# An early check set at a later place, four placing products for eight, and two subtractions on GpSimd

## The chip, the cores and the metric

The kernel runs on one core of a Trainium2 chip. TensorE (PE) multiplies matrices, VectorE (DVE), ScalarE (ACT) and GpSimd (POOL) do the elementwise work, SyncE (SP) and POOL issue transfers. The engines run on their own and meet at semaphores. The metric is the time of the whole program on the device in microseconds; the kernel before takes 439.84 us as the median of three runs (439.14 to 439.93).

## The reference

```python
x = A_x                                   # (1, 2048, 640)
xn = (x - mean(x)) / sqrt(var(x) + 1e-5)   # over the 640 channels
a = einsum("bsd,ed->bse", xn, dft_hid_re);  b = einsum("bsd,ed->bse", xn, dft_hid_im)
A = einsum("ts,bse->bte", dft_seq_re, a) - einsum("ts,bse->bte", dft_seq_im, b)
h = (xn - mean(xn)) / sqrt(var(xn) + 1e-5)
u = gelu(einsum("bsd,sf->bdf", h, w1) + b1)          # F = 1728
B = (einsum("bdf,fs->bds", u, w2) + b2).transpose(0, 2, 1)
out = x + A + B
```

The two DFT matrices along the sequence are 2048 x 2048, the two along the channels 640 x 640; all are inputs. Everything is float32.

## The kernel before

A float32 product is made of three passes in a faster format: each operand is cut into a high half (ACT copies it to the rounded type, `high`, L130) and a low half (DVE subtracts the high half from the source, `low`, L133), and PE multiplies high by high, high by low and low by high (`three`, L138 to L140).

The program is one list of steps. The first 16, called blocks here, take one row tile of x each (128 tokens by 640 channels) in the order of `k_order`, and multiply it with the weight pieces of the first four column groups of w1 into all eight PSUM banks: 24 products a block (`up_pass`, L301). A block needs its row normalized and cut (`row_high`, L245 and L130; `row_low`, L133), and before that the row's moments on DVE (L200, L203), a reciprocal root on ACT (`rooted`, L225) and four tiny instructions that refine it (`factors`, L229 to L232; on DVE for the first five rows, on POOL for the rest). There are 16 early weight pieces of 128 x 512, four for each group of four blocks, in eight buffers (tags h0 to h6 and cut0). The first four are loaded and cut in halves of 256 columns, since they are needed first. After block 15 come the gelus (`gelu`, L325), which read the eight banks on ACT, and step 16, whose products (L138) begin to write the first two of these banks again. Steps 16 and 17 use two further weight pieces ("piece"), cut during blocks 14 and 15.

Since the kernel uses symmetries of the DFT matrices, it checks that they hold: sixteen sets of columns are loaded and compared on DVE with their mirror images (L999, L1003, L1005, L1012), ACT squares what is left and adds it up (L1022), and at the end a verdict decides whether a general version has to run as well. The first seven sets are early ones. Set 0 loads a base and three further tiles of 0.5 MB each through SP; L999 compares the second tile, L1003 the third, L1005 the fourth, and L1012 the base with itself. In the kernel before it is loaded in blocks 4, 4, 5 and 6 and compared three blocks later, with buffers n6 and n7 and the base ck[0].

For the DFT part the row factors of the normalization have to lie in another order of rows: `all_factors` (L398 to L402) computes them for all rows, `norm_parts` cuts them, `norm_products` (L429) multiplies them with four 0/1 matrices on PE, and `norm_places` (L436 and POOL copies) puts them at their places in norm_pairs, which L470 reads later.

The order on each engine is the order in which the program emits its instructions: for every step it runs in turn the loads, the reads of PSUM, the high halves of a piece two steps ahead, the middle, the low half of that piece, the measures and what is to come behind them, and then the step's products. `set_at` puts a set's loads at the steps of a list and its comparisons `by` steps later. Every engine works its list in order, so an instruction that waits holds all behind it.

Of the kernel before, what the change touches and what calls it, by code (L numbers as in the profile page):

```python
# [8 lines left out]
F32 = mybir.dt.float32  # L9
# [3 lines left out]
AF = mybir.ActivationFunctionType  # L13
# [3 lines left out]
P = 128  # L17
S = 2048
D = 640
F = 1728  # L20
NS = S // P
# [18 lines left out]
FIRST = 4  # L40
# [9 lines left out]
def fnet_plus_mixer(  # L50
# [22 lines left out]
    nc = tc.nc  # L73
# [58 lines left out]
    def low(lo, src, hi):  # L132
        nc.vector.tensor_sub(lo, src, hi.bitcast(F32))  # L133
# [63 lines left out]
    def half_moments(k, i):  # L197
        if i == 0:
            stats[k] = small.tile([P, 2, 6], F32, name="st")
        nc.vector.bn_stats(stats[k][:, i, :], rows[k][:, i * H2 : (i + 1) * H2])  # L200
# [222 lines left out]
        low(norm_cut[:, 1], norm, norm_cut[:, 0])  # L423

    def norm_products():
        n = 2 * NS
        for c in range(4):
            for part in range(2):
                nc.tensor.matmul(  # L429
                    psum[6][:, c * n : (c + 1) * n], places[0][:, c // 2, c % 2], norm_cut[:, part].rearrange("p k c -> p (k c)"),  # L430
                    start=c == 0 and part == 0, stop=c == 3 and part == 1, skip_group_check=True,
                )

    def norm_places():
        of = ck[1][:, : 8 * NS]
        nc.scalar.activation(of, psum[6][:, : 8 * NS], AF.Copy)  # L436
        of = of.rearrange("p (s v h k c) -> p s v h k c", s=2, v=2, h=2, k=HS)
        to = norm_pairs.rearrange("p (h b j v) c -> p b v h j c", h=2, b=2, v=2)
        half = P // 2
        for v in range(2):  # L440
            for i in range(2):
                p = slice(half * i, half * (i + 1))
                nc.gpsimd.tensor_copy(to[p, 0, v], of[p, 0, v, :, i : i + 2 * NJ - 1 : 2])

            nc.gpsimd.tensor_copy(to[:, 1, v], of[:, 1, v, :, HS - 2 : HS - 1 - 2 * NJ : -2])
            p = slice(0, half + 1 - v)
            nc.gpsimd.tensor_copy(to[p, 1, v], of[p, 1, v, :, HS - 1 : HS - 2 * NJ : -2])
        nc.gpsimd.tensor_copy(to[0:1, 1, 0], of[0:1, 1, 0, :, NK : NK + 2 * NJ - 1 : 2])
# [582 lines left out]
    def set_at(u, when, by, base, places, late):  # L1031
        load, compare, compare_mirror = seq_set(u, base, places, late)
        for i in range(len(when)):
            at(when[i], load, i, when=loads)
            if i:
                at(when[i] + by, compare, i, when[i] + by, when=behind)
        at(when[-1] + by, compare_mirror, when[-1] + by, when=behind)
# [143 lines left out]
    def early_base(n):  # L1181
        return lambda: ck[(n + 1) % 2][:, : S // 2]
# [4 lines left out]
        return keep.tile([P, S // 2], F32, name=f"check{n}", tag=f"h{4 + i}")  # L1187


    first_ends = []  # L1190

    def first_place(i):
        if i != 1:
            first_ends.append(keep.tile([P, 2, S // 2], F32, name=f"check_first{i}", tag=f"n{6 + i // 2}"))
        return first_ends[-1][:, i % 2]

    set_at(sets[0], [4, 4, 5, 6], 3, early_base(1), first_place, 0)
    for n in range(1, n_early):
        i = n_first + 4 * (n - 1)
        when = [i, i, i + 1, i + 2] if n < n_early - 1 else [i, i, i + 1, i + 4]  # L1200
# [46 lines left out]
    with tc.manual_schedule():  # L1247
        for i in range(2):
            cols = slice(i * H2, (i + 1) * H2)
            nc.sync.dma_start(rows[k_order[0]][:, cols], x_rows[k_order[0]][:, cols])  # L1250
        for n in range(FIRST):
            w1_place(*first_pieces[n])


        def half_pieces(pair, part):
            cols = slice(part * 2 * P, (part + 1) * 2 * P)
            two = w1[2 * pair : 2 * pair + 2, groups[0], :, cols].rearrange("f p c -> p f c")
            nc.sync.dma_start(w_raw[:, pair, :, cols], two)  # L1258

        x_load(k_order[1])  # L1260
        half_pieces(0, 0)
        half_pieces(1, 0)
        for pair in range(2):
            half_pieces(pair, 1)
        for j in range(2, 6):
            x_load(k_order[j])
        for n in range(FIRST, 8):
            w1_load(*first_pieces[n])
        nc.gpsimd.iota(lanes, pattern=[[0, 2]], base=0, channel_multiplier=1)
        constants()  # L1270
        nc.gpsimd.dma_start(b1_sb, b1)
        nc.gpsimd.dma_start(b2_sb, b2)
        iotas()
        nc.scalar.activation(one, eps, AF.Abs_reciprocal_sqrt)

        def first_high(n, part):
            c = slice(part * 2 * P, (part + 1) * 2 * P)
            if part == 0:
                t = early_tile(n)
                w_cut[first_pieces[n]] = t[:, 0], t[:, 1]  # L1280
            high(w_cut[first_pieces[n]][0][:, c], w_at[first_pieces[n]][:, c])

        def first_low(n, part):
            c = slice(part * 2 * P, (part + 1) * 2 * P)
            hi, lo = (a[:, c] for a in w_cut[first_pieces[n]])
            low(lo, w_at[first_pieces[n]][:, c], hi)

        row = k_order[:5]
        moments(row[0])
        rooted(row[0])  # L1290
        factors(row[0])
        row_high(row[0], True)
        for n in range(2):
            first_high(n, 0)
        moments(row[1])
        rooted(row[1])
        for n in range(2, FIRST):
            first_high(n, 0)
        half_low(row[0], 0)
        factors(row[1])  # L1300
        half_low(row[0], 1)
        row_high(row[1], True)
        first_low(0, 0)
        row_low(row[1])
        for n in range(1, FIRST):
            first_low(n, 0)
        mean_by_scalar(row[2])
        variance_by_scalar(row[2])
        rooted(row[2])
        for n in range(FIRST):  # L1310
            first_high(n, 1)
        half_moments(row[3], 0)
        factors(row[2])
        row_high(row[2], True)
        half_moments(row[3], 1)
        joined(row[3])
        row_low(row[2])
        mean_by_scalar(row[4])
        rooted(row[3])
        variance_by_scalar(row[4])  # L1320
        factors(row[3])
        row_high(row[3])
        rooted(row[4])
        for n in range(FIRST):
            first_low(n, 1)
        row_low(row[3])
        factors(row[4])

        for i in range(n_steps + 1):
            j = i + AHEAD  # L1330
            all_of(loads, i)
            if not s_seq <= i < s_hid:
                all_of(reads, i)
            if j < n_steps and steps[j][0]:
                steps[j][0]()
            all_of(reads, i)
            all_of(middle, i)
            if j < n_steps and steps[j][1]:
                ready[j] = steps[j][1]()
            all_of(measures, i)  # L1340
            all_of(behind, i)
            if i < n_steps:
                steps[i][2](ready.pop(i, None))
# [136 lines left out]
```

## Time and profile before

| | |
|---|---|
| median of 3 runs | 439.84 us (439.14 to 439.93) |
| profiled execution, its own time | 439.92 us |
| span from the first to the last instruction | 438.1 us |
| mean granted PE clock | 0.997 |
| PE busy | 430.7 us, 98% |
| DVE busy | 326.1 us, 74% |
| ACT busy | 247.1 us, 56% |
| POOL busy | 108.6 us, 25% |
| blocks 0 to 15 on PE | 7.45 to 66.65 us |

A row of the timeline gives the start, the time taken, the engine, the line, the operation, what is written and read, and in brackets how long the engine stood idle before it and what ended that. A row of the list of waits gives the total in us, the number and the longest. A row of a table of stretches gives the stretch, its length, the busy time of PE with the number of instructions that touch it, the granted clock, the DMA share and GB/s. Matmuls are pipelined: their durations overlap, and the distance between their starts is what a stretch of them costs.

### The profile page before, as it was taken

What the parts mean: (1) busy time and instruction counts of PE and PEld (TensorE: products, weight loads), DVE (VectorE), ACT (ScalarE), POOL (GpSimd) and SP (SyncE); (2) the same over time, 40 slices, a digit from 0 to 9 for tenths busy, and PEclk for the clock granted to TensorE, in tenths of its full rate; (3) what the DMA queues carried; (4) which work ended last, traced back from release to release, by engine and by line L of the source; (5) the groups of instructions that cost most, each with busy time, mean ns of one, the idle gap of its engine ahead of it and who ended that gap; (6) DMA issues with size and microseconds to landing.
All of it is one profiled execution on the core that took longest, in us unless ns stands there. A gap on an engine that the chain in (4) does not pass through costs nothing.

```text
span 438.1 us, 8076 instructions
## 1 busy us (share of the span) xinstructions
PE 430.7 (98%) x2963; PEld 424.4 (97%) x2963; DVE 326.1 (74%) x665; ACT 247.1 (56%) x476; POOL 108.6 (25%) x164
## 2 busy tenths in 40 slices
PE   9999999999999999999999999999999999999994
PEld 5999999999999999999999999999999999999994
DVE  7887861578777777795888759989778677869671
ACT  5967955566556646475946424556645555545540
POOL 2056511032220001100002425546434516312000
PEclk9999999999999999999999999999999999999998
DMA  8992347597886561233203799999999988996301
GB/s 271 339 373 101 104 180 272 178 322 269 279 287 226 194 222 57 72 99 95 101 23 122 212 339 397 389 396 364 404 402 399 399 315 287 407 328 240 113 31 38
DMA packets 43839, 105.68 MB, mean 241 GB/s; under 512 B 5748, under 2 KB 7940, under 8 KB 43792
## 3 DMA queue, kind: packets, MB, share of 16 engines
q1 hardware_dynamic: 34816, 72.66, 46.5%
q0 software_dynamic: 8832, 32.27, 20.2%
q8 instruction: 25, 0.41, 0.4%
q14 instruction: 22, 0.18, 0.1%
q10 hardware_dynamic: 144, 0.16, 0.1%
HBM read 94.58 MB, written 10.49 MB: 240 GB/s over the span
## 4 chain that ended last, share of the span: by engine, by line
PE 87%; DMA 3%; DVE 3%; ACT 2%; POOL 2%; issue 1%; SPq 1%; POOLq 0%; ACTq 0%
PE psum L138 26%; PE psum L140 26%; PE psum L139 26%; PE psum L301 4%; PE psum L897 2%; PE psum L290 2%; DMA xp<-in_x 1%; ACT zt L245 1%; DMA xm<-in_x 1%; POOL r L230 1%; DVE st L200 1%; DVE x L133 1%; DVE early L133 0%; SPq L1258 0%; ACT x L130 0%
## 5 line engine op out<-in xcount | busy, mean ns | idle before, releaser
L133 DVE TENSOR_TENSOR piece<-w_raw,piece 128x512 fp32r<-128x512 f32 (+2 forms) x128 | 76.5, 598 | 80.3 <-ACT piece L130 75.6
L130 ACT ACTIVATE piece<-w_raw 128x512 fp32r<-128x512 f32 (+2 forms) x112 | 67.0, 600 | 110.1 <-PE psum L140 73.4
L138 PE MATMUL psum<-x,piece 128*128 128x320 f32 x288 | 89.1, 309 | 0.0
L140 PE MATMUL psum<-x,piece 128*128 128x320 f32 x288 | 89.1, 309 | 0.0
L139 PE MATMUL psum<-x,piece 128*128 128x320 f32 x288 | 88.8, 308 | 0.0
L1022 ACT ACTIVATE check<-check 128x1024 f32<-128x1024 f32 (+2 forms) x62 | 61.4, 991 | 32.5 <-DVE check L1005 14.2
L140 PE MATMUL psum<-h_cut,piece 128*128 128x320 f32 x256 | 79.2, 310 | 0.0
L138 PE MATMUL psum<-h_cut,piece 128*128 128x320 f32 x256 | 79.1, 309 | 0.0
L139 PE MATMUL psum<-h_cut,piece 128*128 128x320 f32 x256 | 78.8, 308 | 0.0
L301 PE MATMUL psum<-x,early 128*128 128x320 f32 x384 | 58.5, 312 | 1.1 <-DVE x L133 0.4
L301 PEld LDWEIGHTS psum<-x,early 128*128 128x128 f32 x384 | 56.4, 188 | 3.1 <-ACT x L130 1.2
L138 PEld LDWEIGHTS psum<-x,piece 128*128 128x128 f32 x288 | 54.1, 188 | 0.0
L139 PEld LDWEIGHTS psum<-x,piece 128*128 128x128 f32 x288 | 54.1, 188 | 0.0
L140 PEld LDWEIGHTS psum<-x,piece 128*128 128x128 f32 x288 | 54.1, 188 | 0.0
L138 PE MATMUL psum<-h_high,piece 128*128 128x320 f32 x160 | 49.6, 310 | 0.0
L139 PE MATMUL psum<-h_low,piece 128*128 128x320 f32 x160 | 49.4, 309 | 0.0
L140 PE MATMUL psum<-h_high,piece 128*128 128x320 f32 x160 | 49.3, 308 | 0.0
L139 PEld LDWEIGHTS psum<-h_cut,piece 128*128 128x128 f32 x256 | 48.1, 188 | 0.0
L140 PEld LDWEIGHTS psum<-h_cut,piece 128*128 128x128 f32 x256 | 48.1, 188 | 0.0
L138 PEld LDWEIGHTS psum<-h_cut,piece 128*128 128x128 f32 x256 | 48.1, 188 | 0.0
L991 POOL DMA_DIRECT2D check<-in_dft_seq x36 | 26.6, 744 | 16.8 <-ACT check L1022 15.5
L984 POOL DMA_INDIRECT check<-in_dft_seq,from_seq x16 | 19.1, 1191 | 44.8 <-ACT check L1022 41.8
(235 smaller groups left out, 781.7 us busy)
## 6 DMA issues: line engine op xcount, KB each, us to landing
check<-in_dft_seq POOLq DMA_DIRECT2D x36, 512.0 KB
w_raw<-in_w SPq DMA_DIRECT2D x56, 256.0 KB
check<-in_dft_seq SPq DMA_DIRECT2D x18, 512.0 KB
w_raw<-in_w SPq DMA_DIRECT2D x16, 512.0 KB
w_raw<-in_w SPq DMA_DIRECT2D x16, 384.0 KB
rest<-y SPq DMA_DIRECT2D x16, 320.0 KB
rest<-in_x SPq DMA_DIRECT2D x16, 320.0 KB
out<-rest SPq DMA_DIRECT2D x15, 320.0 KB
```

The costliest lines, as they stand in the source:

```text
L130: nc.scalar.activation(hi, src, AF.Copy)
L133: nc.vector.tensor_sub(lo, src, hi.bitcast(F32))
L138: nc.tensor.matmul(bank, wh, mh, start=first, stop=False, skip_group_check=True)
L139: nc.tensor.matmul(bank, wh, ml, start=False, stop=False, skip_group_check=True)
L140: nc.tensor.matmul(bank, wl, mh, start=False, stop=last, skip_group_check=True)
L200: nc.vector.bn_stats(stats[k][:, i, :], rows[k][:, i * H2 : (i + 1) * H2])
L290: nc.tensor.matmul(to[half][:, :H2], w[0][:, c], m[i], start=k == to[2] and i == 0, stop=k == to[3] and i == 1, skip_group_check=True,)
L301: nc.tensor.matmul(up_banks[f][half][:, :H2], w_cut[f, k // G][part == 2][:, c], n[:, part == 1, k % 2, half * H2 : (half + 1) * H2], star ...
L897: nc.tensor.matmul(to, w[0][:, c], m[which], start=False, stop=last and which == 1, skip_group_check=True,)
L984: nc.gpsimd.indirect_dma_start(to[:, c * CH : (c + 1) * CH], None, dft_seq.rearrange("c k p t -> (c k p) t"), bass.IndirectOffsetOnAxis(ap ...
L991: (nc.gpsimd if late else nc.sync).dma_start(to.rearrange("p (c t) -> p c t", c=2), dft_seq[c : c + 2, k + HS * (i // 2)].rearrange("c p t ...
L1022: nc.scalar.activation(v, v, AF.Square, accum_out=off[:, n : n + 1])
```

## The change

Three things. The comparisons of check set 0 move from blocks 7 to 9 to blocks 14 and 15, its loads from blocks 4 to 6 to blocks 11 to 13; its base is now ck[1], and its tiles lie in h0, h1 and h2, the buffers of early weight pieces that block 11 is the last to read. `norm_products` multiplies both halves at once, with 64 columns in four products, and `norm_places` adds the two halves: ACT copies one from PSUM, DVE adds the other. Of the four second low halves of the first weight pieces, two (pieces 2 and 3) are subtracted by POOL, straight behind their high halves, and two stay with DVE.

```diff
     def norm_products():
-        n = 2 * NS
+        n = 4 * NS
         for c in range(4):
-            for part in range(2):
-                nc.tensor.matmul(
-                    psum[6][:, c * n : (c + 1) * n], places[0][:, c // 2, c % 2], norm_cut[:, part].rearrange("p k c -> p (k c)"),
-                    start=c == 0 and part == 0, stop=c == 3 and part == 1, skip_group_check=True,
-                )
+            nc.tensor.matmul(
+                psum[6][:, c * n : (c + 1) * n], places[0][:, c // 2, c % 2], norm_cut.rearrange("p i k c -> p (i k c)"),
+                start=c == 0, stop=c == 3, skip_group_check=True,
+            )
 
     def norm_places():
         of = ck[1][:, : 8 * NS]
-        nc.scalar.activation(of, psum[6][:, : 8 * NS], AF.Copy)
+        both = psum[6][:, : 16 * NS].rearrange("p (s i n) -> p i s n", s=4, i=2)
+        sums = of.rearrange("p (s n) -> p s n", s=4)
+        nc.scalar.activation(sums, both[:, 1], AF.Copy)
+        nc.vector.tensor_add(sums, both[:, 0], sums)
...
-    first_ends = []
-
     def first_place(i):
-        if i != 1:
-            first_ends.append(keep.tile([P, 2, S // 2], F32, name=f"check_first{i}", tag=f"n{6 + i // 2}"))
-        return first_ends[-1][:, i % 2]
-
-    set_at(sets[0], [4, 4, 5, 6], 3, early_base(1), first_place, 0)
+        return keep.tile([P, S // 2], F32, name="check_first", tag=f"h{i}")
+
+    set_at(sets[0], [n_first - 5, n_first - 4, n_first - 4, n_first - 3], 2, early_base(0), first_place, 0)
...
-            low(lo, w_at[first_pieces[n]][:, c], hi)
+            by = nc.gpsimd if part and n > 1 else nc.vector
+            by.tensor_sub(lo, w_at[first_pieces[n]][:, c], hi.bitcast(F32))
...
         for n in range(FIRST):
             first_high(n, 1)
+            if n > 1:
+                first_low(n, 1)
...
-        for n in range(FIRST):
+        for n in range(2):
             first_low(n, 1)
```

How the lists move at two places. First ACT at the end of block 15, where the gelus (h from psum) follow; `piece` is a weight piece of steps 16 and 17. Before:

```order
L130 ACTIVATE x_785<-zt 128x640
L130 ACTIVATE piece<-w_raw 128x512 x2
L398 ACTIVATE q_all<-mv,eps 128x16
L1161 ACT_TABLE_LOAD
L1161 ACTIVATE one<-one 128x1
L325 ACTIVATE h_931<-psum_98,b_sb 128x320
```

and with the change:

```order
L130 ACTIVATE x_774<-zt 128x640
L130 ACTIVATE piece<-w_raw 128x512
L1024 ACTIVATE check_first,off<-check_first 128x1024 x2
L130 ACTIVATE piece<-w_raw 128x512
L398 ACTIVATE q_all<-mv,eps 128x16
L1163 ACT_TABLE_LOAD
L1163 ACTIVATE one<-one 128x1
L1024 ACTIVATE check_first,off<-check_first 128x1024
L1024 ACTIVATE ck_89,off<-ck_89 128x512
L325 ACTIVATE h_932<-psum_98,b_sb 128x320
```

Two squares of the set now stand ahead of the second piece and of q_all, and two between them and the first gelu.

Second DVE in blocks 14 and 15, from the last rows' low halves on (lane and places_of make the 0/1 matrices, low_c, low_d and good are another check). Before:

```order
L133 TENSOR_TENSOR x_785<-zt,x_785 128x640 x2
...
L133 TENSOR_TENSOR piece<-w_raw,piece 128x512
L399 SCALAR_TENSOR_TENSOR r_all<-mv,q_all 128x16
...
L1103 TENSOR_REDUCE low_c<-ck_88 4x1
...
L133 TENSOR_TENSOR piece<-w_raw,piece 128x512
L967 MEMSET mirror 1x1
```

and with the change:

```order
L133 TENSOR_TENSOR x_774<-zt,x_774 128x640 x2
...
L133 TENSOR_TENSOR piece<-w_raw,piece 128x512
L1001 SCALAR_TENSOR_TENSOR check_first<-ck_89,parity,check_first 128x1024
L1005 TENSOR_TENSOR check_first<-ck_89,check_first 128x512 x2
L399 SCALAR_TENSOR_TENSOR r_all<-mv,q_all 128x16
...
L1105 TENSOR_REDUCE low_c<-ck_88 4x1
...
L133 TENSOR_TENSOR piece<-w_raw,piece 128x512
L1007 SCALAR_TENSOR_TENSOR check_first<-ck_89,parity,check_first 128x512 x2
L1014 SCALAR_TENSOR_TENSOR ck_89<-ck_89,parity 128x512
L969 MEMSET mirror 1x1
```

The first two comparisons stand ahead of L399, which reads q_all from ACT, the last two behind the low half of the second piece.

## The prediction

> **What bounds the kernel now.** I read the page first, then the list of what PE waited for, then stretches of 4 us, then the timeline.
>
> ```profile
> span 438.1 us, 8076 instructions
> PE 430.7 (98%) x2963; PEld 424.4 (97%) x2963; DVE 326.1 (74%) x665; ACT 247.1 (56%) x476; POOL 108.6 (25%) x164
> ...
> PE psum L301 <- DVE x L133: 0.4, 1, 0.4
> ...
> 40.00:44.00 4.00, 3.48 (x22) 1.00 0.00 0
> ...
> 48.00:52.00 4.00, 3.62 (x25) 1.00 0.29 78
> 52.00:56.00 4.00, 4.00 (x29) 1.00 0.97 323
> ```
>
> PE bounds the kernel: 430.7 of 438.1 us. All its waits after the warm-up stand at L301, the first blocks. A stretch of 4 us with no wait holds 29 matmuls (52 to 56 us), but 40 to 44 holds 22 and 48 to 52 holds 25: 11 lost. The step between matmuls is 0.145 us (three starts from 66.65 to 66.94 below), so 1.6 us is lost there. Nothing later on PE takes up a delay of the first blocks: what they lose or win moves the end. What holds them is seen in the timeline:
>
> ```profile
> 33.47 0.72 POOL L230 TENSOR_SCALAR r<-r,q 128x1 f32<-128x1 f32 x1 [1.81 <-ACT q L225]
> ...
> 37.00 1.76 POOL L230 TENSOR_SCALAR r<-r,q 128x1 f32<-128x1 f32 x1 [1.37 <-ACT q L225]
> 37.42 1.29 DVE L999 SCALAR_TENSOR_TENSOR check_first<-ck,parity,check_first 128x1024 f32<-128x1024 f32 x1
> ...
> 39.52 0.92 ACT L245 ACTIVATE zt<-xp,again 128x640 f32<-128x640 f32 x1 [1.99 <-POOL again L232]
> ...
> 41.99 1.29 DVE L1003 TENSOR_TENSOR check_first<-ck,check_first 128x512 f32<-128x512 f32 x2
> ...
> 44.45 1.05 ACT L1022 ACTIVATE check_first<-check_first 128x1024 f32<-128x1024 f32 x1
> 45.49 0.62 ACT L130 ACTIVATE early<-w_raw 128x512 fp32r<-128x512 f32 x1
> 45.53 1.41 DVE L1005 SCALAR_TENSOR_TENSOR check_first<-ck,parity,check_first 128x512 f32<-128x512 f32 x2
> ...
> 46.20 0.91 ACT L245 ACTIVATE zt<-xp,again 128x640 f32<-128x640 f32 x1
> ...
> 46.98 0.75 DVE L1012 SCALAR_TENSOR_TENSOR ck<-ck,parity 128x512 f32<-128x512 f32 x1
> ...
> 47.78 1.05 ACT L1022 ACTIVATE check_first<-check_first 128x1024 f32<-128x1024 f32 x1
> ...
> 48.82 0.62 ACT L1022 ACTIVATE ck<-ck 128x512 f32<-128x512 f32 x1
> ```
>
> The check set's four DVE steps (c1 L999, c2 L1003 twice, c3 L1005 twice, c4 L1012) and their ACT squares (L1022) stand between the rows' work. POOL's tiny L230 ends 0.05 us after c1 does: it was held, by 1.04 us over its 0.72 of the row before, and block 9's row (L245 at 39.52) waited for it.
>
> **The check set, moved.** Without c1 that row starts at 39.52 - 1.04 = 38.48, and the 1.6 us of PE waits go: PE could begin step 16 at 66.65 - 1.6 = 65.05. But step 16 writes the PSUM banks that the gelus (L325) empty, and ACT's list now has two squares ahead of them, with c3 and c4 behind everything else on DVE. What stands there now:
>
> ```profile
> 56.91 0.92 ACT L245 ACTIVATE zt<-xm,again 128x640 f32<-128x640 f32 x1 [0.94 <-POOL again L232]
> ...
> 58.51 1.14 ACT L130 ACTIVATE piece<-w_raw 128x512 fp32r<-128x512 f32 x2
> 58.63 0.83 DVE L133 TENSOR_TENSOR x<-zt,x 128x640 fp32r<-128x640 f32 x1 [1.81 <-ACT x L130]
> ...
> 59.55 0.29 ACT L398 ACTIVATE q_all<-mv,eps 128x16 f32<-128x16 f32 x1
> ...
> 61.12 0.17 DVE L399 SCALAR_TENSOR_TENSOR r_all<-mv,q_all 128x16 f32<-128x16 f32 x1
> ...
> 64.60 0.06 DVE L967 MEMSET mirror<- 1x1 int32 x1
> ...
> 65.83 0.53 ACT L325 ACTIVATE h<-psum,b_sb 128x320 f32<-128x320 f32 x1 [4.47 <-PE psum L301]
> 66.65 0.31 PE L138 MATMUL psum<-x,piece 128*128 128x320 f32 x1
> ...
> 66.94 0.31 PE L140 MATMUL psum<-x,piece 128*128 128x320 f32 x1
> ```
>
> The new schedule by these rows, starts in us:
> - ACT, rows 9 to 15. Row 9 takes 1.58 (46.20 to 47.78), so ACT is free at 40.06. A row with its weight piece takes 2.29 (45.49 to 47.78); four of them, rows 10 to 13, reach 49.22. Row 14 has no piece: 2.29 less 0.57 (1.14 for two at 58.51) is 1.72, to 50.94; row 15 takes 1.58 and 0.1 for its last end: 52.6 if POOL never holds it. Before, row 15 waited 0.94 for POOL: 53.6. I take the middle-to-late 53.2.
> - DVE. From the last row's L133 to L399 it took 61.12 - 58.63 = 2.49, so it reaches c1 at 53.2 + 2.49 = 55.7, and c1 and c2, 1.29 each, end at 58.3. ACT's second square follows, 1.05; then the high half of piece 17, 0.57, and q_all, 0.29: 60.3 with hand-overs. Only then does L399 run, so 2.0 us of DVE pass empty. L399 to L967 took 64.60 - 61.12 = 3.48, to 63.8; c3, 1.41, then ends at 65.2, and c4 at 66.0 (45.53 to 46.98 + 0.75 is 2.20 for both).
> - ACT's squares: 65.3 to 66.3 and, 0.62, to 67.0. The first gelu takes 0.53: 67.5. PE follows at about 67.55, against 66.65 before: **+0.9**, and 0.1 for the first matmul after a wait. PE stands idle from 65.05 to 67.55, 2.5 us.
>
> So the waits removed at 40 to 52 us come back as one of 2.5 us at step 16: +1.0 on the path. Without any POOL wait it is +0.4; with row 15 at 53.6 and 0.1 more for each row, +1.7. The set's four loads (0.5 MB each) leave the crowded time before 35 us and are issued from about 50 us, when block 11 frees their tiles; c1 comes 5 us later, and 52 to 56 us moved 323 GB/s, 0.5 MB in 1.6 us. They stand ahead of four weight pieces and a pair of x loads on SP, none of which step 16 or 17 needs. No gain on PE is counted for them: no wait above names a DMA.
>
> **The 0/1 products.**
>
> ```profile
> 73.68 0.96 PE L429 MATMUL psum<-norm_cut,places_of 128*128 128x32 f32 x8
> 74.49 0.39 PE L138 MATMUL psum<-x,piece 128*128 128x320 f32 x1
> ...
> 83.27 0.92 ACT L470 ACTIVATE xp<-xp,norm_pairs 128x640 f32<-128x640 f32 x1
> ```
>
> Eight take 74.49 - 73.68 = 0.81, 0.101 each. Four with 64 columns cost at least 0.101 and, by the 320-column step, at most 0.147 each: they save 0.22 to 0.41. A 32-column product that costs two thirds of a 320-column one is paid for its weights, so I take **-0.4**. The added DVE sum of the two halves (some 0.5 us) delays the POOL copies that follow; norm_pairs is first read at 83.27, so 8 us cover it; beyond them each us late would delay ACT's scaling of the rows by as much.
>
> **The two low halves on POOL.**
>
> ```profile
> 12.21 1.33 ACT L130 ACTIVATE early<-w_raw 128x256 fp32r<-128x256 f32 x4
> ...
> 14.38 0.82 DVE L133 TENSOR_TENSOR x<-zt,x 128x640 fp32r<-128x640 f32 x1
> ...
> 16.06 1.42 DVE L133 TENSOR_TENSOR early<-w_raw,early 128x256 fp32r<-128x256 f32 x4
> ...
> 17.91 0.83 DVE L133 TENSOR_TENSOR x<-zt,x 128x640 fp32r<-128x640 f32 x1 [0.43 <-ACT x L130]
> ...
> 234.34 0.46 POOL L806 TENSOR_TENSOR y_mid<-y_mid 2x161 f32<-2x161 f32 x1
> ...
> 234.77 0.70 POOL L807 TENSOR_TENSOR y_mid<-y_mid 2x161 f32<-2x161 f32 x1
> ```
>
> DVE loses two of the four at 16.06, 0.7 us, and gains nothing: it waits for ACT before 17.91 anyway. POOL does its two from 13.2 on (third of the four ACT pieces). By its rows, 0.46 and 0.70 for 161 elements, one takes 0.7 to 1.1; both end before 16.5, and PE needs them from 17.7. The cost is in what DVE loses if POOL holds it: nothing, if POOL's work falls before and after the L133 at 14.38; 1.0 if that L133 waits for a whole one. The chain from there to row 9 has no slack, so that passes on whole. I take **+0.2**, since the one measured case of holding (37.00) has POOL as the one that waits.
>
> The Trainium skill, "SBUF — State Buffer", section "Who interferes with whom", says that DVE instructions with two SBUF inputs and a GpSimd instruction that reads SBUF exclude each other for a whole instruction, and that the order of issue decides who waits. By that DVE can lose as well, and the term would be up to 1.0. The trace agrees for POOL as the loser (1.76 against 0.72 us); no row has DVE as the loser.
>
> **The sum.** The profiled execution took 439.92 us, 0.08 above the median, its span 438.1. 439.92 + 1.0 - 0.4 + 0.2 = **440.7**.
>
> **The rivals.**
> - *The clock falls in the gap: 442.3.* The rows below show the warm-up at 11 matmuls of 512 columns in 4.3 us, then 17 in 2.1, and at the end, with no matmul from 432.70 on, the granted clock is 1.00 to 435.10 and 0.50 after 435.30: it halves some 2.5 us into a gap. A gap of 2.5 us is at that edge. The way back took 4.3 us at half rate, so it costs up to 2.1; I take 1.6. Against it: the gap has to fall rightly, and the gaps at 40 to 52 us, 1.0 together at most, did nothing (clock 1.00 there).
>
> ```profile
> 0.78:5.10 4.32, 4.32 (x11) 1.00 0.71 201
> 5.10:7.23 2.13, 2.13 (x17) 1.00 1.00 291
> ...
> 432.70:435.10 2.40, 0.00 (x0) 1.00 0.43 146
> ...
> 435.30:438.10 2.80, 0.00 (x0) 0.50 0.08 17
> ```
>
> The Trainium skill, "TensorE: Matmul & The Clock Gate", Part 1, has the clock judged in free-running windows of 3.4 us; by that it would cost half a window, 1.7, whenever one is mostly idle. The trace agrees in that it fell 2.5 us, not 0, after the end.
> - *POOL holds DVE for a whole subtraction: 441.5.* The 0.2 becomes 1.0. For it: nothing keeps them apart at 14.38. Against: only POOL is seen waiting.
> - *No wait at step 16: 439.92 - 1.6 - 0.4 = 437.9.* The other side, and what the change would give alone. It needs the gelus by 65.0, 2.0 us before 67.0. Against it: of the 13.8 us from row 15's x to the first gelu, only the 2.0 us that DVE waits for q_all are not work, and row 15 can't come before 52.6.
> - *The two cancel: 439.6.* Rows 14 and 15 never wait for POOL and DVE's list is 0.3 us shorter than its rows.
>
> **How the numbers follow.** Forecast 0.50 (its own range 440.0 to 441.7); clock 0.22; POOL 0.10; no wait 0.09; cancel 0.09. The range 439.2 to 442.6 leaves out "no wait" and the upper part of the clock's case. Faster or slower counts from 0.2%, 0.88 us from 439.84, about what a measurement can tell: the forecast lies at that edge, so it gives 0.22 slower and 0.28 same; the clock 0.21 slower, POOL 0.09, the rest of both same, "cancel" 0.08 same and 0.01 faster, "no wait" 0.09 faster.
>
> **What would show it.** Right: no PE wait between 36 and 60 us, c3 starting near 63.8, an idle ACT before its square at about 65.3, the first L325 near 67.0, a PE wait of some 2.5 us on ACT just before step 16, and L429 at 0.4 us. The clock case: a granted clock of 0.5 in 66 to 71 us. POOL: DVE's L133 of 14.38 starting 0.5 us or more later. Wrong at its root: gelus that start by 65 us, or rows 9 to 15 slower than 2.3 us each on ACT.

## The result and the profile after

The changed kernel takes 446.0 us (445.91 to 446.06) against 439.88 us for the kernel before on the same chip: a ratio of 1.0139, with a 95% interval of 1.0125 to 1.0153. One further execution of it, and one of the kernel of experiment 1, was disturbed and is left out. The forecast was 440.7 us with a range of 439.2 to 442.6: slower was right, but the loss is 6 us and not 1. The profiled execution took 445.91 us, its span 444.1, against 439.92 and 438.1 before.

First the page of the changed kernel, its span and busy times, and then its list of what PE waited for (total, number of times, longest).

```profile
span 444.1 us, 8076 instructions
PE 431.4 (97%) x2959; PEld 426.0 (96%) x2959; DVE 326.4 (73%) x664; ACT 247.4 (56%) x476; POOL 110.8 (25%) x166
```

```profile
PE psum L138 <- ACT h L325: 4.3, 1, 4.3
PE psum L301 <- ACT early L130: 1.2, 1, 1.2
PE psum L127 <- PEq L1470: 0.8, 1, 0.8
```

The waits of the first blocks at 40 to 52 us are gone, as forecast: what is left at L301 is at the start of block 0 (1.2 us, 0.2 before). In their place stands one wait at step 16 (L138) on the gelus (L325), also as forecast, but of 4.3 us and not 2.5. What it set off is seen in the stretches around it (stretch, length, busy time and count of PE, weight loads, DVE, ACT, POOL, granted clock, DMA share, GB/s):

```profile
72.00:76.00 4.00, 4.00 (x19) 4.00 (x18) 0.69 (x1) 1.23 (x3) 0.00 (x0) 0.58 0.80 294
...
65.37:68.55 3.18, 0.16 (x2) 0.00 (x0) 2.92 (x10) 0.94 (x1) 0.00 (x0) 1.00 0.66 233
68.55:75.37 6.82, 5.54 (x21) 5.54 (x22) 0.69 (x1) 4.68 (x13) 0.00 (x0) 0.50 0.90 320
75.37:77.00 1.63, 1.63 (x13) 1.63 (x13) 0.18 (x1) 0.63 (x1) 0.00 (x0) 1.00 0.38 141
```

The last product of block 15 starts at 65.22 and ends at 65.53; the next could have started one step later than it, at 65.37. From there to 69.83 PE has nothing to start: a gap of 4.46 us, counted like this here and below. The granted clock falls to 0.50 at 68.55 and is back at 75.37; 72 to 76 us hold 19 products where an undisturbed stretch of 4 us holds 29 or 30. So the rival "the clock falls in the gap" came true together with the forecast's own wait, and both are larger than they were priced.

The timeline of the changed kernel, rows 9 to 15 and what follows (start, time taken, engine, line, and in brackets the idle time ahead and what ended it). The set's lines are c1 L1001, c2 and c3 L1005 and L1007, c4 L1014, squares L1024:

```profile
38.87 0.93 ACT L245 ACTIVATE zt<-xp,again 128x640 f32<-128x640 f32 x1 [0.95 <-POOL again L232]
...
42.38 1.43 POOL L232 TENSOR_SCALAR again<-mv,again 128x1 f32<-128x1 f32 x1
43.84 0.92 ACT L245 ACTIVATE zt<-xp,again 128x640 f32<-128x640 f32 x1 [0.28 <-POOL again L232]
...
45.52 0.92 POOL L231 TENSOR_SCALAR again<-r,q 128x1 f32<-128x1 f32 x1
...
46.84 0.92 ACT L245 ACTIVATE zt<-xm,again 128x640 f32<-128x640 f32 x1 [0.60 <-POOL again L232]
...
48.52 0.93 POOL L232 TENSOR_SCALAR again<-mv,again 128x1 f32<-128x1 f32 x1
...
49.48 0.92 ACT L245 ACTIVATE zt<-xm,again 128x640 f32<-128x640 f32 x1 [0.24 <-POOL again L232]
...
50.96 0.26 POOL L232 TENSOR_SCALAR again<-mv,again 128x1 f32<-128x1 f32 x1
52.98 0.82 DVE L133 TENSOR_TENSOR x<-zt,x 128x640 fp32r<-128x640 f32 x1 [0.95 <-ACT x L130]
52.99 0.95 POOL L232 TENSOR_SCALAR again<-mv,again 128x1 f32<-128x1 f32 x1
53.97 0.93 ACT L245 ACTIVATE zt<-xm,again 128x640 f32<-128x640 f32 x1 [1.03 <-POOL again L232]
...
55.70 0.83 DVE L133 TENSOR_TENSOR x<-zt,x 128x640 fp32r<-128x640 f32 x1 [1.90 <-ACT x L130]
...
58.19 1.28 DVE L1001 SCALAR_TENSOR_TENSOR check_first<-ck,parity,check_first 128x1024 f32<-128x1024 f32 x1
59.38 1.29 DVE L1005 TENSOR_TENSOR check_first<-ck,check_first 128x512 f32<-128x512 f32 x2
...
60.75 1.06 ACT L1024 ACTIVATE check_first<-check_first 128x1024 f32<-128x1024 f32 x1
...
62.33 0.29 ACT L398 ACTIVATE q_all<-mv,eps 128x16 f32<-128x16 f32 x1
...
62.65 0.17 DVE L399 SCALAR_TENSOR_TENSOR r_all<-mv,q_all 128x16 f32<-128x16 f32 x1 [1.99 <-ACT q_all L398]
...
66.13 1.40 DVE L1007 SCALAR_TENSOR_TENSOR check_first<-ck,parity,check_first 128x512 f32<-128x512 f32 x2
67.56 0.75 DVE L1014 SCALAR_TENSOR_TENSOR ck<-ck,parity 128x512 f32<-128x512 f32 x1
67.61 1.06 ACT L1024 ACTIVATE check_first<-check_first 128x1024 f32<-128x1024 f32 x1 [3.47 <-issue]
68.66 0.61 ACT L1024 ACTIVATE ck<-ck 128x512 f32<-128x512 f32 x1
69.27 3.43 ACT L325 ACTIVATE h<-psum,b_sb 128x320 f32<-128x320 f32 x8
69.83 0.63 PE L138 MATMUL psum<-x,piece 128*128 128x320 f32 x1 [4.30 <-ACT h L325]
...
79.46 0.53 PE L428 MATMUL psum<-norm_cut,places_of 128*128 128x64 f32 x4
...
437.43 0.30 PE L899 MATMUL psum<-h_low,piece 128*128 128x320 f32 x1
```

Read from the bottom up, each link is the forecast's: the gelus begin when the second of the last two squares lets ACT go, the squares wait for c3 and c4 (ACT's 3.47 us before 67.61 are put down to "issue", but this square reads what c3 writes, and c3 ends at 67.53), these stand on DVE behind L399, which stood idle 1.99 us for q_all, and q_all stands on ACT behind the first two squares.

The six us of span, from the rows above and those of before (start of step 16 at 66.65, products at 73.68 to 74.49, last matmul at 432.32):

| stretch | before | after | difference |
|---|---|---|---|
| start of step 16 | 66.65 | 69.83 | +3.18 |
| step 16 to the 0/1 products | 7.03 | 9.63 | +2.60 |
| the 0/1 products, up to the next L138 | 0.81 | 0.37 | -0.44 |
| from there to the last matmul | 357.83 | 357.60 | -0.23 |
| last matmul to the end of the span | 5.8 | 6.7 | +0.9 |

### The profile page after: what moved, and what is told of

The parts are those of the page before. It is cut to its first block, busy times and chain, and to the rows that moved or that the text cites. A ratio compares the mean times of both kernels' runs of the same rounds, so it can differ in the third digit from the quotient of the medians.

```text
span 444.1 us, 8076 instructions
## 1 busy us (share of the span) xinstructions
PE 431.4 (97%) x2959; PEld 426.0 (96%) x2959; DVE 326.4 (73%) x664; ACT 247.4 (56%) x476; POOL 110.8 (25%) x166
## 4 chain that ended last, share of the span: by engine, by line
PE 96%; DMA 1%; issue 1%; ACT 0%; SPq 0%; DVE 0%; ACTq 0%
PE psum L138 26%; PE psum L139 26%; PE psum L140 26%; PE psum L301 13%; PE psum L290 2%; PE psum L899 2%; DMA w_raw<-in_w 1%; SPq L1248 0%; PE psum L377 0%; DVE rest L919 0%; SPq L193 0%; ACT early L130 0%; ACT h L325 0%; PE psum L428 0%; PE psum L653 0%
## 5 line engine op out<-in xcount | busy, mean ns | idle before, releaser
L133 DVE TENSOR_TENSOR piece<-w_raw,piece 128x512 fp32r<-128x512 f32 (+2 forms) x128 | 76.5, 597 | 78.8 <-ACT piece L130 74.7
L138 PE MATMUL psum<-x,piece 128*128 128x320 f32 x288 | 90.3, 314 | 4.3 <-ACT h L325 4.3
L139 PE MATMUL psum<-x,piece 128*128 128x320 f32 x288 | 90.0, 312 | 0.0
L140 PE MATMUL psum<-x,piece 128*128 128x320 f32 x288 | 89.9, 312 | 0.0
L1024 ACT ACTIVATE check<-check 128x1024 f32<-128x1024 f32 (+2 forms) x62 | 61.4, 992 | 32.6 <-DVE check L1007 14.2
L138 PE MATMUL psum<-h_cut,piece 128*128 128x320 f32 x256 | 79.0, 308 | 0.0
L138 PEld LDWEIGHTS psum<-x,piece 128*128 128x128 f32 x288 | 55.1, 191 | 4.6 <-ACT h L325 4.6
L301 PE MATMUL psum<-x,early 128*128 128x320 f32 x384 | 57.8, 311 | 1.2 <-ACT early L130 1.2
L301 PEld LDWEIGHTS psum<-x,early 128*128 128x128 f32 x384 | 56.4, 188 | 2.5 <-ACT early L130 1.5
L139 PEld LDWEIGHTS psum<-x,piece 128*128 128x128 f32 x288 | 55.1, 191 | 0.0
L140 PEld LDWEIGHTS psum<-x,piece 128*128 128x128 f32 x288 | 55.1, 191 | 0.0
L138 PE MATMUL psum<-h_high,piece 128*128 128x320 f32 x160 | 49.4, 309 | 0.0
L138 PEld LDWEIGHTS psum<-h_cut,piece 128*128 128x128 f32 x256 | 48.1, 188 | 0.0
L139 PEld LDWEIGHTS psum<-h_low,piece 128*128 128x128 f32 x160 | 30.1, 188 | 0.0
```

The source lines that it names most:

```text
L138: nc.tensor.matmul(bank, wh, mh, start=first, stop=False, skip_group_check=True)
L139: nc.tensor.matmul(bank, wh, ml, start=False, stop=False, skip_group_check=True)
L140: nc.tensor.matmul(bank, wl, mh, start=False, stop=last, skip_group_check=True)
L301: nc.tensor.matmul(up_banks[f][half][:, :H2], w_cut[f, k // G][part == 2][:, c], n[:, part == 1, k % 2, half * H2 : (half + 1) * H2], star ...
L1024: nc.scalar.activation(v, v, AF.Square, accum_out=off[:, n : n + 1])
```

## The experiments

S is the theory that step 16 waits for the set's last squares, since these stand ahead of the gelus on ACT, and that the idle time then halves the clock. Where a rival is named D or otherwise, its condition and numbers stand beside it. Each ratio is to the kernel before on the same chip.

**1. The set's move alone.**

```diff
-    set_at(sets[0], [4, 4, 5, 6], 3, early_base(1), first_place, 0)
+    set_at(sets[0], [n_first - 5, n_first - 4, n_first - 4, n_first - 3], 2, early_base(0), first_place, 0)
```

(and first_place as in the change; nothing else of the change.)

> Only the check set is moved; the eight products and DVE's four low halves are as before. Theory S (the gelus stand on ACT behind the set's last two squares, step 16 waits for them, and the wait is long enough to halve PE's clock): about 446.2 us, that is all of the 6 us lost plus the 0.4 us of the products; a PE wait of 4 to 4.6 us on ACT before step 16 and a granted clock of 0.5 behind it. Rival P (POOL's two subtractions hold DVE and the whole row chain, and the set only adds a little): 440 to 442 us.

Measured: ratio 1.0121 (1.0103 to 1.0140), 444.8 to 445.6 us; S had 446.2, P 440 to 442. Its waits and the stretch with the low clock:

```profile
PE psum L138 <- ACT h L325: 4.2, 1, 4.2
```

```profile
67.44:74.26 6.82, 4.49 (x17) 4.50 (x18) 1.51 (x7) 5.62 (x13) 0.00 (x0) 0.50 1.04 370
```

The same wait and the same low clock, for the same 6.82 us. The set's move alone brings 5.3 us of the loss (1.0121 of 439.82). The changed kernel loses 0.8 us more, of which 0.7 lie behind the last matmul (6.0 us here, 6.7 there; see 8), and the two intervals overlap.

**2. The four products alone.**

```diff
-        n = 2 * NS
+        n = 4 * NS
```

(with the one product of 64 columns and the sum of the halves, as in the change.)

> Only the four products for eight. Both theories: 0.4 us less than before (the trace of the changed kernel has 0.37 us for the four against 0.81 for the eight), 439.4 us; no other difference.

Measured: 439.49 us, ratio 0.9991 (0.9982 to 1.0000). That is at the edge of what can be told from nothing; the profile has the products at 73.92 and the next L138 at 74.28, 0.36 us against 0.81.

**3. The two low halves on GpSimd alone.**

```diff
-            low(lo, w_at[first_pieces[n]][:, c], hi)
+            by = nc.gpsimd if part and n > 1 else nc.vector
+            by.tensor_sub(lo, w_at[first_pieces[n]][:, c], hi.bitcast(F32))
```

(with the two calls at their new places.)

> Only the two low halves on POOL. Theory S: within 0.5 us of before, 439.8 to 440.4 us: DVE's low half of row 2 lasts 1.36 us in place of 0.82, and most of it is caught in DVE's idle time before row 3. Rival P: at least 442 us.

Measured: 440.84 us, ratio 1.0020 (1.0011 to 1.0029). This part costs some 0.9 us by itself, but the profile doesn't show it on the way to the last matmul, which starts at 432.44 against 432.32. The span is 0.9 us longer, and 0.7 us of that lie behind the last matmul. More of that under 8.

**4. The last two squares behind the gelus.** The changed kernel with one condition more; the comparisons stay where they are on DVE.

```diff
-            if late:
+            if late or (u == sets[0] and i in (0, 3)):
                 at(step + 1, run, when=measures)
```

> The whole change, with the set's last two squares put behind the eight gelus on ACT; DVE's list is the same. Theory S: no wait at step 16, no half clock, and the change gives what it removes: 1.6 us of waits and 0.4 us of products, so 438.0 to 438.6 us. Rival D (DVE's longer list or the later pieces decide at step 16, not the gelus): still 442 us or more, with a PE wait before or in steps 16 and 17.

Measured: 438.13 us, ratio 0.9961 (0.9947 to 0.9975): 7.9 us less than the changed kernel and 1.7 us less than the kernel before. Its waits on PE, the gelus and the start of step 16:

```profile
PE psum L127 <- PEq L1470: 0.8, 1, 0.8
PE psum L301 <- ACT early L130: 0.5, 2, 0.3
```

```profile
63.76 3.46 ACT L325 ACTIVATE h<-psum,b_sb 128x320 f32<-128x320 f32 x8 [0.47 <-ACT one L1163]
...
64.53 0.31 PE L138 MATMUL psum<-x,piece 128*128 128x320 f32 x1
...
65.28 1.40 DVE L1007 SCALAR_TENSOR_TENSOR check_first<-ck,parity,check_first 128x512 f32<-128x512 f32 x2
```

The gelus now run before c3 does, and no wait is left at step 16, which starts at 64.53. Two squares of 1.7 us on ACT, moved past the gelus, undo the whole loss; that is the step of the chain that S names, and D is out, since DVE's list is the same. The last matmul starts at 429.53, 2.8 us before that of the kernel before: 0.7 of it was there at the start of block 0 (6.74 against 7.45 in these two executions), 0.4 are the 0/1 products, and some 1.6 are the waits that the set's move removes.

**5. Filling the gap: first try.** The clock's part of the loss is separated from the wait's by giving PE something to do. 75 products on constants go into columns of a PSUM bank that nobody reads; apart from them the kernel is the changed one.

```diff
         def products(w, f=f, g=g):
+            for _ in range(75 if (f, g) == (FIRST, 0) else 0):
+                nc.tensor.matmul(psum[7][:, 384 : 384 + 128], idle[:, :P], idle[:, :128], start=True, stop=True, skip_group_check=True)
             for k in range(g * G, (g + 1) * G):
```

> 75 products of 128 columns on constants, into 128 columns of a PSUM bank that nobody reads, stand ahead of step 16 and keep TensorE busy while it waits for the gelus; the wait itself is not touched. S (the set's last squares hold the gelus, and the idle time halves the clock): step 16 starts within 0.3 us of the changed kernel's 69.83, the granted clock stays 1.00 from 65 to 80 us, the way from step 16 to the norm products is 7.0 us instead of 9.6, and the time is about 443.3 (442.8 to 444.0). Rival, the clock does not cost the 2.6 us (step 16 is slow for another reason): about 446.0, with the 9.6 us still there.

Measured: 452.22 us, ratio 1.0270 (1.0254 to 1.0285); neither expectation. The edit did not do what it was to do, as the wait on PE and the stretches of the low clock and of step 16 show:

```profile
PE psum L339 <- ACT h L325: 7.2, 1, 7.2
```

```profile
70.44:77.25 6.81, 4.48 (x43) 4.48 (x43) 0.69 (x1) 2.80 (x7) 0.00 (x0) 0.50 0.79 271
79.11:86.13 7.02, 7.02 (x52) 7.02 (x49) 0.69 (x1) 0.63 (x1) 0.00 (x0) 1.00 0.00 0
```

The added products were issued behind the gelus, and waited for the last of them, which reads the same bank in other columns; the wait grew to 7.2 us. It still tells two things: the clock was low for 6.81 us again, though the gap was longer (7.4 us from 65.37 on), and once it is back at 1.00, step 16 to the 0/1 products takes 7.0 us.

**6. Filling the gap: second try.** The same 75 products, now issued behind step 15's own and so ahead of the gelus.

```diff
                 for i in range(2):
                     up_pass(k_order[i], 2)
+            if j == len(k_order) - 1:
+                for _ in range(75):
+                    nc.tensor.matmul(psum[7][:, 384 : 384 + 128], idle[:, :P], idle[:, :128], start=True, stop=True, skip_group_check=True)
```

> The 75 products on constants now stand behind step 15's own products and are issued before the gelus, so that they do not wait for any of them; by the 2.5 us that some 42 of them took at full clock elsewhere (0.059 each, an estimate) they last about 4.4 us, the length of the gap. S (the gap halves the clock and that costs 2.6 us): step 16 starts at 69.8 to 70.3, the granted clock is 1.00 from 64 to 80 us, step 16 to the norm products takes 7.0 us instead of 9.6, and the time is about 443.4 (442.8 to 444.2). Rival, the 9.6 us belong to something else than the clock: 446.0 with the 9.6 us still there.

Measured: 443.12 us (442.85 to 444.08), ratio 1.0071 (1.0054 to 1.0088). The stretch of the added products, and that from step 16 to the 0/1 products:

```profile
65.83:70.30 4.47, 4.47 (x77) 4.42 (x76) 2.92 (x10) 2.23 (x6) 0.00 (x0) 1.00 0.76 255
70.30:77.44 7.14, 7.14 (x52) 7.14 (x49) 1.38 (x2) 4.03 (x9) 0.00 (x0) 1.00 0.85 285
```

Step 16 starts no earlier (70.30 against 69.83), but the clock stays at 1.00 and the way to the products takes 7.14 us instead of 9.63. The program is 2.9 us shorter for 75 useless products. So of the 6 us some 2.5 are the clock's, and the rest is the later start and the end.

**7. The roots of all factors first.** The changed kernel with `all_factors` one step earlier: q_all stands ahead of the set's first two squares on ACT, and with it DVE's four tiny instructions that use it (L399 to L402) move ahead of c1.

```diff
-    at(n_first - 1, all_factors)
+    at(n_first - 2, all_factors)
```

> The changed kernel with the roots of all factors (q_all) one step earlier on ACT, ahead of the set's first two squares there; nothing else moves. S (the chain of row 15, c1 and c2, their squares, q_all, c3, c4, last squares, gelus is what step 16 waits for): VectorE's wait of 2.0 us for q_all goes, step 16 starts about 2.0 us earlier, near 67.8 (67.3 to 68.4), its wait shrinks from 4.3 to 2.3 to 2.6 us, and the time is about 444.0 if the clock still halves, 441.5 to 442.7 if it does not. Rival, the gelus wait for something else: the wait stays above 3.8 us and the time within 0.5 of 446.0.

Measured: 441.33 us (440.68 to 442.84), ratio 1.0039 (1.0025 to 1.0053). The wait on PE, the gap with the products after it, and the links of the chain:

```profile
PE psum L138 <- ACT h L325: 2.1, 1, 2.1
```

```profile
65.13:67.40 2.27, 0.16 (x3) 0.00 (x1) 0.80 (x5) 2.23 (x6) 0.00 (x0) 1.00 0.80 235
67.40:71.00 3.60, 3.60 (x24) 3.60 (x25) 0.17 (x1) 3.39 (x8) 0.00 (x0) 1.00 1.04 390
```

```profile
63.47:66.88 3.41, 1.82 (x13) 1.55 (x11) 2.42 (x8) 2.62 (x7) 0.00 (x0) 1.00 0.68 197
66.88:70.29 3.41, 2.89 (x19) 2.89 (x20) 0.00 (x0) 3.41 (x10) 0.00 (x0) 1.00 0.98 365
```

```profile
63.68 1.41 DVE L1007 SCALAR_TENSOR_TENSOR check_first<-ck,parity,check_first 128x512 f32<-128x512 f32 x2
...
66.84 3.43 ACT L325 ACTIVATE h<-psum,b_sb 128x320 f32<-128x320 f32 x8
67.40 0.41 PE L138 MATMUL psum<-x,piece 128*128 128x320 f32 x1 [2.11 <-ACT h L325]
```

One tiny activation of 0.29 us in another place, with four instructions of 0.2 us behind it on DVE, moves c3 by 2.45 us (66.13 to 63.68) and step 16 by 2.43 (69.83 to 67.40): the chain from c3 to step 16 passes a delay on whole. And the gap of 2.27 us left the clock at 1.00 in the profiled execution, where gaps of 4.4 to 4.5 us halved it in the changed kernel, with the set alone and in the last kernel of 8, and one of 7.4 us in 5. Three of the nine executions took 442.4 to 442.8 us; their mean granted clocks were 0.991 to 0.995, those of the other six 0.995 to 0.998. Whether the clock fell in them at the gap, no trace shows. The second pair of stretches, 3.41 us each, is used below, under the clock.

**8. What lies behind the last matmul.** Two kernels ask whether GpSimd's two subtractions lengthen the end. The first is that of 4 with all low halves on DVE, the second the one of 3 with two memsets of one column on DVE in the subtractions' old places.

```diff
-            by = nc.gpsimd if part and n > 1 else nc.vector
-            by.tensor_sub(lo, w_at[first_pieces[n]][:, c], hi.bitcast(F32))
+            low(lo, w_at[first_pieces[n]][:, c], hi)
```

> The set moved, its last two squares behind the gelus, four products for eight, and all low halves on DVE again. If the two subtractions on GpSimd cost the 0.7 to 0.9 us that the kernels with them have more behind the last matmul: 437.3 to 437.6. Rival, the longer end belongs to something else (or the subtractions win as much as they cost): 438.1 as with them.

```diff
         for n in range(2):
             first_low(n, 1)
+            nc.vector.memset(spare[:, n : n + 1], 0.0)
```

> The kernel before with the two subtractions on GpSimd, and two memsets of one column on VectorE in the places that the subtractions left, so that VectorE has as many instructions as before. If the longer end comes from VectorE's shorter program (where its last instructions lie): about 440.0, the end as short as before. If it comes from GpSimd's two instructions or from the time of the early blocks: 440.8 as without the memsets.

Measured: 438.43 us, ratio 0.9961 (0.9948 to 0.9975), for the first, the same as with GpSimd, as the rival has it; 440.34 us, ratio 1.0011 (1.0002 to 1.0020), for the second, between its two expectations. There the end is short again, but the last matmul starts at 433.06, 0.6 us later than in 3. The changed kernel itself with all low halves on DVE was run too:

> The changed kernel with all low halves on DVE. The gap at step 16 is set by rows 9 to 15, c1 to c4 and the squares, not by the early low halves: step 16 within 0.4 us of 69.83, clock halved there as before. If the two subtractions on GpSimd cost nothing on the path and the longer end is not theirs: 445.6 to 446.2. If they cost what the kernel with them alone had over the kernel before (0.9 us): about 445.1.

It took 444.96 us (443.9 to 446.54), ratio 1.0107 (1.0087 to 1.0127). Its profiled execution has step 16 at 69.95 and the clock at 0.50 again; the ratio is 0.3% under the changed kernel's, and the spread of its executions is too wide to say whether GpSimd's part makes the difference. They sort by the mean granted clock: 443.9 us at 0.995, 444.45 at 0.991, 445.47 at 0.989, 446.54 at 0.988, so the spread may be the clock's.

The time from the start of the last matmul to the end of the span falls into two groups: 5.5 us in the second kernel, 5.6 in that of 2, 5.8 in the kernel before, 6.0 in that of 1; 6.5 to 6.8 in all others, the first kernel here (without GpSimd's subtractions) among them. So the subtractions are not needed for the long end, and the second kernel shows that they don't bring it by themselves.

The traces also show where the time goes. At the program's end each engine branches past the general version (L1438 before) and then works off a closing list. Counted from the start of the last matmul, SyncE starts that list at 3.28 us in the kernel before and at 3.25 to 3.72 in the other three with a short end, but at 4.42 in the changed kernel and at 4.26 to 4.53 in all others with a long end, except that of 3. There SyncE has 3.28, and it is VectorE that starts its list late, at 5.41, against 3.90 to 4.42 in every other kernel. The late start goes with the place of the branch in the engine's own list: SyncE is late wherever it has 335 recorded instructions ahead of its branch and not where it has 330, 331 or 336; VectorE is late with 831 and not with 832 to 834. Two subtractions less took VectorE to 831 in 3, and the two memsets took it back to 833, as the second kernel's first expectation had it. In the changed kernel it is SyncE that moved, from 331 to 335 (336 with the set alone). Why one place costs more than its neighbours was not tried.

The cost of GpSimd's part alone lies between nothing (4 against the first kernel here) and 0.9 us (3).

## Why the prediction was right or wrong

**The mechanism: right.** The waits of 40 to 52 us go, and one wait at step 16 takes their place, through the links named: c1 and c2, first squares, q_all, DVE's 2.0 us without work (measured 1.99), c3 and c4, last squares, gelus. The removed waits were sized rightly too: from the start of block 0 to the gap PE takes 57.61 us (7.76 to 65.37) where it took 59.20, 1.59 less for the 1.6 that was forecast. Experiment 1 has it in the set's move alone, 4 and 7 at two of its links.

**The size of the +1.0: wrong, by its first link, and by the clock that follows from it.** The step that failed is the schedule of rows 9 to 15 on ACT, which put the last row's L133 at 53.2. It starts at 55.70, 2.5 us later. From there on every duration of the forecast holds within some 0.2 us: q_all ends at 62.62 (60.3 forecast), c3 starts at 66.13 (63.8), the first gelu at 69.27 (67.0), PE at 69.83 (67.55), each 2.3 us late. The forecast took the row's pace from ACT's own work and let POOL hold it only in row 15, for 0.6 of the 0.94 us that it had there before. In the trace after, ACT waits for POOL's tiny L232 in four of rows 10 to 15, 0.28, 0.60, 0.24 and 1.03 us, 2.15 in all. L232 takes 0.26 where nothing holds it (50.96) and 0.93 to 1.43 in three of the four, where DVE is in its L133 with two inputs (42.38, 48.52, 52.99; L133 at 52.98); in the fourth it is L231 ahead of it that takes 0.92, where it takes 0.27 elsewhere (45.52). Every profiled kernel with the set moved has the same four waits to within 0.05 us, and the kernel before only that of row 15. So without c1 to c4 between them, DVE's L133 of one row falls on POOL's factors of a next one; this is read from the traces, and no run keeps the two apart. That moved work would bring new holds was seen for DVE, not for the rows that it left behind. Row 9 itself began 0.4 us after its forecast 38.48 (0.3 of it since the first rows, 14.68 against 14.38 for the L133 shown below), and the rest is ACT's rows, some 0.5 us longer in all. The bound given, +1.7 "with row 15 at 53.6 and 0.1 more for each", was too near: it counted 0.1 for each row where 0.2 to 1.0 was measured in four of them, and by its own terms, 0.4 and seven times 0.1 on top of the +1.0, it should have read +2.1.

**The clock: a rival with a wrong condition.** It was priced for a gap of 2.5 us, at the edge of where the clock falls, and given 0.22. Experiment 7, with 2.27 us, is nearly the case that was forecast: it starts step 16 at 67.40 (67.55 forecast), keeps its clock in the profile and takes 441.3 us, of which 0.7 us are the longer end. One profile doesn't show that 0.22 was right. With gaps of 4.4 us and more the clock fell in all four profiled executions. Its price was short as well: 1.6 was forecast, 2.6 measured (9.63 less 7.03), and 6 confirms it from the other side (7.14 at full clock). The granted clock is low for 6.82 us, of which 5.54 fall on products; at half rate these cost half of that, 2.8. The forecast had taken 4.3 us, the length of the warm-up at the start.

The clock goes by fixed windows in these traces: between any two of its changes in one trace lies a whole number of 3.413 us (64.853 us, 19 of them, from the first rise to the fall in the changed kernel; 61.440, 18, in 1). The low stretches of 6.81 to 6.82 us in the changed kernel and in 1 and 5 are two such windows, and they begin 3.0, 1.9 and 4.9 us after the last product's end, so the fall isn't counted from the gap's start. The window ahead of the fall need not be empty: in 1 PE worked in 1.49 of its 3.41 us (64.03 to 67.44). And in 7 the gap lay across two windows, with 1.82 and 2.89 us of work left in them, and the clock stayed up. So the place of a gap may count beside its length, and 7 may owe its full clock to its place; no run moves the gap alone. The forecast's half window was wrong: the window in which PE came back, with 2.13 us of work in the changed kernel, did not bring the clock back either, and only the next, full one did.

The Trainium skill, "TensorE: Matmul & The Clock Gate", Part 1, says that activity is judged in free-running windows of 3413 ns, and that the clock rises only after a busy one. The traces agree, with 6.82 us for two of them.

**The 0/1 products: right.** 0.37 against 0.81 us, -0.44 for -0.4; nothing waits for norm_pairs.

**The two low halves: right on the path, not in the sum.** DVE did lose, where the trace before had shown only POOL as the one that waits. Three rows of the changed kernel, and then one instruction in the kernel before and in the changed one:

```profile
13.61 1.75 POOL L1285 TENSOR_TENSOR early<-w_raw,early 128x256 fp32r<-128x256 f32 x2 [10.35 <-ACT early L130]
...
14.68 1.36 DVE L133 TENSOR_TENSOR x<-zt,x 128x640 fp32r<-128x640 f32 x1
...
18.75 0.83 DVE L133 TENSOR_TENSOR x<-zt,x 128x640 fp32r<-128x640 f32 x1 [1.09 <-ACT x L130]
```

```profile
19.36 0.27 DVE L230 TENSOR_SCALAR r<-r,q 128x1 f32<-128x1 f32 x1 [0.55 <-ACT early L130]
...
19.75 0.27 DVE L230 TENSOR_SCALAR r<-r,q 128x1 f32<-128x1 f32 x1
```

L133 took 1.36 us instead of 0.82 and passed that on to the next row: its L133 starts at 18.75 instead of 17.91, 0.84 us later, of which 0.30 was there before the hold (14.68 against 14.38). DVE's 1.09 us ahead of it don't catch the delay, since ACT itself had waited for DVE's factors there. It is caught one row on, at L230: the kernel before stood 0.55 us idle there, the changed one not at all, and only 0.39 us of lateness are left. (The Trainium skill, "SBUF — State Buffer", section "Who interferes with whom", has either engine as the one that waits; here both are seen, POOL with 1.76 us for 0.72 and DVE with 1.36 for 0.82.) In 3 another instruction was held, L247 with 0.93 us instead of 0.62, and not the L133 that its expectation names; there the last matmul is 0.1 us later for +0.2 forecast. The 0.9 us that the part costs alone lie mostly behind the last matmul, where the forecast counted nothing.

**The end: not foreseen.** 0.9 us behind the last matmul, in no term and no rival. In the changed kernel it goes with the place of SyncE's branch (see 8), which nothing in the change aims at.

Together, from 440.7: 2.3 us more at step 16's start, 2.6 for the clock and 0.9 at the end, less 0.6 in the smaller terms (0.2 on GpSimd not found on the path, 0.1 for the first matmul, 0.2 between the products and the last matmul, the rest rounding), make 445.9.

**The rival on the other side** ("no wait at step 16", 437.9) names what the change would have been worth. Experiment 4 built it: 438.13. In its profiled execution an end 0.8 us longer than before and a first block 0.7 us earlier offset each other, so that the nearness is in part luck.

## What to carry to other kernels

Before moving work behind a stretch that feeds PE, follow each engine's list to the next thing that PE waits for: here two squares of 1.7 us, and the comparisons that they wait for, ahead of the gelus make the change lose 6 us, and with the squares behind the gelus the same change wins 1.7. When removed work is used to speed up a chain of tiny instructions, forecast the pace from what those instructions take beside the work that stays (L232 0.26 alone, 0.93 to 1.43 held), not from the busiest engine's sum. A PE wait of 4 us is not paid by its length alone: here it brought 2.6 us of half clock, and filling it with useless products won back 2.9.

## What the runs showed of the hardware that was not expected

- The granted clock was low for 6.81 to 6.82 us after a single gap in each of three kernels whose gaps were 4.4, 4.5 and 7.4 us long: the length of the low stretch did not follow the gap's. It need not always be that long: the executions of 444.78 us in 1 and 443.9 us in 8 have a mean granted clock of 0.995, which leaves room for 5 us of half clock at most, the program's end included (an estimate from these means).
- A product that writes columns 384 to 511 of a PSUM bank stood still until an activation had read columns 0 to 319 of it (7.2 us in 5). Whether the order comes from the program's own bookkeeping or from the bank was not tried.
- The end behind the last matmul is 5.5 to 6.0 us in some kernels and 6.5 to 6.8 in others, with the same last instructions. GpSimd's subtractions don't sort them. In all twelve traces the long end goes with the place of the branch ahead of the closing list, on SyncE (335 recorded instructions ahead of it) or VectorE (831). Why is open.
